# TensorE's queue order in a fused attention and mixture kernel: the attention product of a group placed behind the scores of the group four further on

## The chip, the cores and the metric

The kernel runs as one program on one core of a Trainium2 chip. The metric is the device time of one execution in microseconds (us); several executions are timed and the median is given. One further execution was recorded by the hardware profiler, and all rows below come from that one.

## The reference

Three stages follow each other. Attention with a top-k mask: for each of 4 batches and 8 heads, with 576 positions of width 64, only the 32 largest scores of a row stay.

```python
scores = scale * np.matmul(q, k.transpose(0, 1, 3, 2))
kth = np.partition(scores, -top_k, axis=-1)[..., -top_k:-top_k + 1]
scores = np.where(scores >= kth, scores, -1000000000.0)
attn = softmax(scores);  x = np.matmul(attn, v)
```

Then a dense block over the 2304 tokens: `h = x @ w_in` (512 to 2048), softplus, `@ w_out` (2048 to 512). Then a mixture of 8 experts of which each token takes one: `argmax` of `x @ w_gate`, and for the chosen expert `relu(x @ w1[e]) @ w2[e]` times the gate's probability.

## The kernel before, in words

Part one (`part_one`) does attention and the dense block interleaved, part two (`part_two`, from about 805 us of the profile on) the experts. Part two and the end of the dense block are not touched.

Attention is cut into 72 **groups** of two tiles, each tile 128 query rows of one head (or 64 and 64 rows, a "tail"). Two neighbouring heads of a batch are a pair; a pair's queries, keys and values sit in one of 4 buffers. A group j goes through these steps:

- **Scores**, `emit_qk`, L372 on TensorE: 8 to 12 matmuls into the PSUM tile `s`, of which there is one buffer. ScalarE copies it to SBUF (L380).
- **Softmax with top-k**, `emit_softmax`: VectorE folds the row into halves and quarters (L408 to L424; L424 is the last reader of the PSUM tile, so it sets the scores of group j+1 free), finds the 32nd largest value with pairs of L428 and L432, and makes the mask (L443, or L440, which multiplies at once). GpSimd multiplies by the mask (L444), ScalarE and GpSimd write the two float16 halves of the weights into `p16` (L448 to L450), and the SP queue transposes them by DMA into `pT` (L452). There are six `pT` buffers, the tiles of three groups.
- **The attention product**, `emit_av`, L467 and L469 on TensorE: 14 matmuls per tile with `pT` as the weights into the PSUM tile `m`, of which there is one buffer. VectorE makes the reciprocal of the row sums (L491, L493) and ScalarE writes the scaled rows `x` (L495).

Of `x` a **unit** of two tiles of 128 tokens is made for the dense block: ScalarE and GpSimd split it into float16 halves `xh` (L514, L515), the SP queue transposes it into `xT` (L516), and 16 **steps** follow, each of 12 matmuls of the first layer (L554) and 2 of the second (L588, or L585 for the last unit, recorded as two each). Behind a unit stands the routing of its tokens (L592 to L656).

What sets the order: the Python loop of `part_one` writes, at turn i, the scores of group i+1, the softmax of group i, the product of group i-3 (`LAG = 3`) and one or two steps of the dense block. A list scheduler then places all instructions on the five engines by priority and by a simulated time line. `tc.high_priority(offset=A_AV)` around the product (A_AV = 150; the scores have 100) lets it go ahead of much that was written earlier. Each engine executes its own list strictly in the order that results, and stops at an instruction whose operands are not there.

The scheduler places a product on TensorE as soon as it holds the transposed weights to be there. In the list that results product j stands mostly behind the scores of group j+2, with one group's turn between the end of its softmax and its place.

The names that the change and the steps of the prediction touch: `last_qk`, `emit_qk` (L372), `emit_av` (L467 to L495), the loop at the end of `part_one`.

Of the kernel before, what the change touches and what calls it, by code (L numbers as in the profile page):

```python
# [19 lines left out]
B, H, S, D = 4, 8, 576, 64  # L20
# [54 lines left out]
A_AV = 150  # L75
# [12 lines left out]
def attn_moe_moe2(ctx, tc, q, k, v, w_in, w_out, w_gate, w1, w2, out):  # L88
# [64 lines left out]
    def run(halves):  # L153
        nc.vector.memset(done, 0.0)
        with ExitStack() as p:
            late = part_one(tc, p, q, k, v, w_in, w_out, const, ident, before, ones, iota_e, reg_e, wg, ids,
                            ohcum, done, early, table, rows, flags if halves else None, sums, w_sums)
        with ExitStack() as p:
            part_two(tc, p, w1, w2, out, ident, ones, ohcum, done, early, late, table, rows, check if halves else None)
# [10 lines left out]
def part_one(tc, ctx, q, k, v, w_in, w_out, const, ident, before, ones, iota_e, reg_e, wg, ids,  # L170
             ohcum, done, early, table, rows, flags, sums, w_sums):
    nc = tc.nc
# [100 lines left out]
    def decode_some(n):  # L273
        for _ in range(n):
            if dec_q:
                f, *a = dec_q.pop(0)
                f(*a)
# [6 lines left out]
    def prep_load(m):  # L284
        b, hp = pairs[m]
        src = []
        bd = sm.tile([128, 3], F32, name="bd") if flags is None else sums[:, m]
        for i, x in enumerate((q, k, v)):
            t = raw.tile([128, R * D], F32, name="qkv"[i] + "n")
            nc.sync.dma_start(t, x[b, 2 * hp:2 * hp + 2].rearrange("h (p r) d -> (h p) (r d)", r=R))  # L290
            src.append(t)
        pair[m] = (src, bd)
        if flags is None or m >= LATEJ:
            magnitudes(m)
# [7 lines left out]
    def prep_scale(m):  # L302
        b = pairs[m][0]
        src, bd = pair[m]
        if flags is not None:
            return
        up, iv = pow2(all_sum(bd, ps_m, "m"), "m")
        sc = sm.tile([128, 8], F32, name="sc", bufs=KVB + 2)
        nc.vector.tensor_copy(sc[:, 0:3], up)
        nc.vector.tensor_tensor(out=v_up[:, b:b + 1], in0=v_up[:, b:b + 1], in1=up[:, 2:3], op=ALU.min)  # L310
        nc.vector.scalar_tensor_tensor(sc[:, 3:4], iv[:, 0:1], 1.0 / D ** 0.5, iv[:, 1:2],
                                       op0=ALU.mult, op1=ALU.mult)
        nc.vector.tensor_scalar(sc[:, 4:5], sc[:, 3:4], -1.0, None, op0=ALU.mult)
        for i in (1, 0, 2):
            nc.scalar.activation(src[i], src[i], AF.Copy, scale=sc[:, i:i + 1])
        pair[m] = (*src, sc)
# [36 lines left out]
        pair[m] = (q1, q2, kt, v16, sc)  # L353

    sc_t, pt_t, o_t, x_t = {}, {}, {}, {}
    tops = [None]

    def emit_qk(m, kind, ps, base):
        q1, q2, kt, v16, sc = pair[m]
        if kind == "tail":  # L360
            parts = [(8, 9, h, 64 * h, 64 * h + 64) for h in range(2)]
        else:
            t, h = kind
            parts = [(2 * t, 2 * t + 2, h, 0, 128)]

        cut = (512 * (base // 512 + 1) - base) // D
        for r0, r1, h, p0, p1 in parts:
            cs = slice(h * 64, h * 64 + 64)
            for qs, first in ((q1, True), (q2, False)):
                lhs = qs[:, h, r0:r1, :].rearrange("p r d -> p (r d)")  # L370
                for k0, k1 in ((0, cut), (cut, R)):
                    nc.tensor.matmul(ps[p0:p1, base + k0 * D:base + k1 * D], lhsT=lhs, rhs=kt[:, k0:k1, cs],  # L372
                                     start=first, stop=not first)

    def emit_scores(gi):
        s = row.tile([128, 2, S], F32, name="s")
        ps = ps_s.tile([128, 1536], F32, name="s")
        for i, x in enumerate(groups[gi]):
            emit_qk(*x, ps, i * S)
        nc.scalar.activation(s.rearrange("p i c -> p (i c)"), ps[:, 0:2 * S], AF.Copy)  # L380
        sc_t[gi] = s, ps
# [78 lines left out]
    def emit_av(m, kind):  # L460
        b, hp = pairs[m]
        v16, sc = pair[m][3:5]
        pT = pt_t.pop((m, kind))
        def products(o, pT, h):
            for r in range(R):
                c = r if r < 5 else r - 5
                nc.tensor.matmul(o[:, h, 0:D + 1], lhsT=pT(r), rhs=v16[:, h, c, 0:D + 1], start=r == 0, stop=r == R - 1)  # L467
                if r < 5:
                    nc.tensor.matmul(o[:, h, 0:D], lhsT=pT(r), rhs=v16[:, h, c, D + 2:], start=False, stop=False)  # L469

        def out_tile():
            return ps_m.tile([128, 512], F32, name="m")[:, :2 * D + 4].rearrange("p (h c) -> p h c", h=2)

        if kind == "tail":
            o = out_tile()
            p0 = 64 * (b % 2)
            for h in range(2):
                products(o[p0:p0 + 64], lambda r: pT[:, r, h * 64:h * 64 + 64], h)
            xt, ps_ = x_tile((b // 2, "tail%d" % (b // 2))), slice(p0, p0 + 64)
        else:  # L480
            t, h = kind
            if h == 0:
                o_t[m, t] = out_tile()
            o = o_t[m, t]
            products(o, lambda r: pT[:, r, :], h)
            if h == 0:
                return
            del o_t[m, t]
            xt, ps_ = x_tile((b, t)), slice(0, 128)
        rc = sm.tile([128, 2, 1], F32, name="rc")  # L490
        nc.vector.tensor_scalar(rc[ps_], o[ps_, :, D:D + 1], ESC * 1e-9,  # L491
                                2.0 ** -X_UP if flags is not None else sc[ps_, 2:3], op0=ALU.add, op1=ALU.mult)
        nc.vector.reciprocal(rc[ps_], rc[ps_])  # L493
        for h in range(2):
            nc.scalar.activation(xt[ps_, hp, h], o[ps_, h, 0:D], AF.Copy, scale=rc[ps_, h])  # L495
# [103 lines left out]
    def some_work(k):  # L599
        for _ in range(k):  # L600
            moe_step()
            if side:
                next(side[0], None)
                if side[0].gi_frame is None:
                    side.pop(0)
# [113 lines left out]
    pairs, tiles, first = [], [], []  # L719
# [18 lines left out]
    n = len(groups)  # L738
# [4 lines left out]
    for i in range(-1, n + LAG):  # L743
        if i == -1:
            with tc.high_priority(offset=AHEAD):
                for m in range(RB):
                    prep_load(m)
                prep_scale(0)
        while done_prep < len(pairs) and when[done_prep] <= i:
            with tc.high_priority(offset=A_PREP):  # L750
                if to_scale:
                    prep_scale(to_scale.pop()[0])
                prep_split(done_prep)
                if done_prep + RB < len(pairs):
                    prep_load(done_prep + RB)
                if done_prep + 1 < len(pairs):
                    to_scale.append((done_prep + 1, i + SCALE))
            done_prep += 1
        if to_scale and to_scale[0][1] <= i:
            with tc.high_priority(offset=AHEAD):  # L760
                prep_scale(to_scale.pop()[0])
        if i == -1:
            decode_some(2)
        if i + 1 < n:
            with tc.high_priority(offset=A_SC):
                emit_scores(i + 1)
        if 0 <= i < n:
            with tc.high_priority(offset=AHEAD):
                emit_softmax(i)
            with tc.high_priority(offset=0):  # L770
                decode_some(DECR)
        j = i - LAG
        if j >= 0:
            with tc.high_priority(offset=A_AV):
                for x in groups[j]:
                    emit_av(*x)
            for u in units.get(j, []):
                started += 1
                ready.append((u, started))
        if ready or cur or behind or side:  # L780
            credit += MOER
            some_work(int(credit))
            credit -= int(credit)
# [267 lines left out]
```

## Time and profile before

| | us |
|---|---|
| median of 3 runs | 1141.56 |
| lowest and highest run | 1136.7, 1143.85 |
| the profiled execution's own time | 1135.44 |
| its span, first to last instruction | 1133.7 |
| mean granted TensorE clock, share of full | 0.929 |

Three stretches can be told apart. Up to about 250 us the kernel also decodes the dense block's weights on VectorE, ScalarE and GpSimd. From 250 to about 805 us the rest of attention runs with the dense block beside it. From 805 us on come the last units and the experts, in which TensorE is busy throughout. The view "busy time by stretch" shows how much an engine does in a stretch, the view of waits what it stood still for, and the time line which instruction stood and which one ran on.

### The profile page before, as it was taken

To read this page: it belongs to the slowest core of one execution; us is meant where nothing else is said; L and a number is where in the kernel's file an instruction comes from. 1 tells how busy PE (TensorE), PEld (TensorE's weight loads), DVE (VectorE), ACT (ScalarE), POOL (GpSimd) and SP (SyncE) were. 2 spreads that over 40 slices of the span, in tenths; PEclk is the share of its full clock that TensorE was granted. 3 is DMA by queue.
4 is the path that set the end of the run, shared out by engine and by line. 5 is a ranking of instruction groups with operands and counts; after the bars stand their busy time and mean duration, and the time that the engine had idled before them with its cause. 6 is when DMAs were issued, how large, how long until landed. Compare 5 with 4: busy or idle time off the path is not lost. (4 is left out here: it accounts for less than half of the span.)

```text
span 1133.7 us, 22612 instructions
## 1 busy us (share of the span) xinstructions
PE 902.4 (80%) x7146; PEld 648.5 (57%) x7146; DVE 951.6 (84%) x2980; ACT 800.5 (71%) x1898; POOL 638.4 (56%) x731
## 2 busy tenths in 40 slices
PE   1233367757898797789988998998999999999992
PEld 0122244434565464556655565665678889999981
DVE  4998999999898897799988998999656787677771
ACT  6776688877677778687987776867679655555561
POOL 3986898987666677566767765656434112111110
PEclk9995589877999999899999998999999999999996
DMA  8897778975748877546769543354521566766650
GB/s 194 190 199 157 148 166 197 205 157 112 98 100 131 147 117 148 91 63 102 140 146 134 93 78 71 73 73 92 188 39 21 105 248 201 249 221 235 211 188 18
DMA packets 295880, 157.18 MB, mean 139 GB/s; under 512 B 257524, under 2 KB 257652, under 8 KB 295732
## 3 DMA queue, kind: packets, MB, share of 16 engines
q1 hardware_dynamic: 292116, 145.73, 60.1%
q0 software_dynamic: 3616, 9.72, 2.5%
q8 instruction: 62, 1.02, 0.4%
q14 instruction: 86, 0.70, 0.3%
HBM read 77.89 MB, written 11.11 MB: 79 GB/s over the span
## 5 line engine op out<-in xcount | busy, mean ns | idle before, releaser
L588 PE MATMUL y<-w_out_s,g 128*128 128x512 f32 x480 | 238.8, 618 | 11.3 <-POOL g L563 11.3
L554 PE MATMUL h<-xT,w_in_s 128*128 128x256 f16 (+1 forms) x1920 | 231.5, 270 | 9.1 <-ACT g L560 4.7
L554 PEld LDWEIGHTS <-w_in_s 128*128 128x128 f16 x1920 | 173.4, 101 | 77.0 <-issue 52.9
L432 DVE MAX8 mx<-wk 128x8 f32<-128x144 f32 (+2 forms) x432 | 198.5, 493 | 0.1
L467 PE MATMUL m<-v,pT 128*128 128x65 f16 (+1 forms) x1440 | 104.5, 203 | 103.4 <-DMA pT<-p 88.1
L563 POOL TENSOR_TENSOR g<-g,sa 128x256 f32<-128x256 f32 (+1 forms) x160 | 118.3, 741 | 108.2 <-ACT sa L562 95.9
L450 POOL TENSOR_TENSOR p<-e,p 128x512 f16<-128x512 f32 x144 | 169.1, 1174 | 0.0
L372 PE MATMUL s<-kt,q 128*128 128x512 f16 (+7 forms) x640 | 104.3, 326 | 76.9 <-DVE wk L424 52.2
L467 PEld LDWEIGHTS <-pT 128*128 128x128 f16 (+1 forms) x1440 | 91.4, 108 | 120.3 <-DMA pT<-p 107.5
L444 POOL TENSOR_TENSOR e<-e,mk 128x576 f32<-128x576 f32 x84 | 110.9, 1322 | 63.5 <-DVE mk L443 47.7
L428 DVE MATCH_REPLACE8 wk<-mx,wk 128x144 f32<-128x144 f32 (+1 forms) x432 | 144.3, 339 | 0.1
L448 ACT ACTIVATE p<-e 128x576 f16<-128x576 f32 x144 | 98.1, 682 | 53.3 <-DVE e L440 19.5
L588 PEld LDWEIGHTS y<-w_out_s,g 128*128 128x128 f32 x480 | 84.1, 198 | 73.1 <-issue 54.1
L870 POOL DMA_INDIRECT out_dram<-ot,idx x19 | 19.8, 1045 | 177.8 <-DVE ot L869 159.2
L372 PEld LDWEIGHTS <-q 128*128 128x128 f16 (+1 forms) x640 | 46.7, 110 | 124.5 <-issue 47.9
L890 PEld LDWEIGHTS h<-xT,wf 128*128 128x128 f32 x864 | 111.9, 191 | 5.3 <-ACT wf L851 0.2
L890 PE MATMUL h<-xT,wf 128*128 128x256 f32 x864 | 114.0, 283 | 0.0
L903 PE MATMUL y<-wf,hT 128*128 128x512 f32 x432 | 112.6, 398 | 0.0
L421 ACT ACTIVATE e<-s,bias 128x576 f32<-128x576 f32 x144 | 105.6, 770 | 1.6 <-POOL p L450 0.8
L380 ACT ACTIVATE s<-s 128x1152 f32<-128x1152 f32 x72 | 81.0, 1125 | 6.6 <-PE s L372 6.4
L903 PEld LDWEIGHTS y<-wf,hT 128*128 128x128 f32 x432 | 76.7, 189 | 13.2
L469 PE MATMUL m<-v,pT 128*128 128x64 f16 (+1 forms) x800 | 80.4, 203 | 0.0
(193 smaller groups left out, 1907.3 us busy)
## 6 DMA issues: line engine op xcount, KB each, us to landing
w1r<-in_moe_w_dram SPq DMA_DIRECT2D x20, 1024.0 KB, 5.1
w2r<-in_moe_w_dram SPq DMA_DIRECT2D x20, 1024.0 KB, 6.5
w<-in_moe_w_in_dram SPq DMA_DIRECT2D x16, 512.0 KB, 5.2
w<-in_moe_w_out_dram SPq DMA_DIRECT2D x16, 512.0 KB, 4.3
rows<-xr SPq DMA_DIRECT2D x37, 128.2 KB, 2.5
qn<-in_q_dram SPq DMA_DIRECT2D x16, 288.0 KB, 3.2
kn<-in_k_dram SPq DMA_DIRECT2D x16, 288.0 KB, 3.2
vn<-in_v_dram SPq DMA_DIRECT2D x16, 288.0 KB, 3.3
```

Source lines behind the costliest of these rows:

```text
L372: nc.tensor.matmul(ps[p0:p1, base + k0 * D:base + k1 * D], lhsT=lhs, rhs=kt[:, k0:k1, cs], start=first, stop=not first)
L421: nc.scalar.activation(e[i], s[i], AF.Exp, bias=bt[:, i], scale=SCORE if flags is not None else sc[i][:, 3:4])
L428: nc.vector.match_replace(out=to, in_to_replace=mx[:, i, 8 * j:8 * j + 8], in_values=src[i], imm_value=NEG)
L432: nc.vector.max(out=mx[:, i, 8 * j + 8:8 * j + 16], in_=src[i])
L444: nc.gpsimd.tensor_tensor(out=e[i], in0=e[i], in1=mk, op=ALU.mult)
L450: nc.gpsimd.tensor_tensor(out=p16[:, S + D:], in0=e[i][:, 0:S - D], in1=p16[:, 0:S - D], op=ALU.subtract)
L467: nc.tensor.matmul(o[:, h, 0:D + 1], lhsT=pT(r), rhs=v16[:, h, c, 0:D + 1], start=r == 0, stop=r == R - 1)
L554: nc.tensor.matmul(hps[:, :n], lhsT=w_in_s[:, c, j, p, o:o + 128], rhs=xT[:, 0:len(u.tiles), r, c, :], start=m == 0, stop=m == 3 * KD - 1)
L563: nc.gpsimd.tensor_tensor(out=g, in0=g, in1=a[:, :n], op=ALU.add)
L588: nc.tensor.matmul(u.y[i], lhsT=g[:, cs], rhs=w_out_s[:, f, :], start=f == 0, stop=f == KF - 1)
L890: nc.tensor.matmul(h, lhsT=w1f[:, a, c, :], rhs=xT[:, b, c, :], start=n == 0, stop=n == 3 * KD - 1)
L903: nc.tensor.matmul(y[i], lhsT=hT[g][:, a, i * 128:i * 128 + 128], rhs=w2f[:, b, :], start=g == 0 and n == 0, stop=g == KF2 - 1 and n == 2)
```

## The change

The product of group j = i-3 is now issued behind the last score matmul of group i+1 = j+4 on TensorE: `emit_qk` keeps its latest matmul in `last_qk`, and the block that writes the product is entered with `tc.issue_after(...)`. That adds an edge for order alone from that matmul to each instruction of the block on the same engine; no semaphore is added by it. Products 68 to 71 have no scores four further on (the loop's test `i + 1 < n`) and stand behind the last ones. Nothing is computed otherwise.

```diff
-    tops = [None]
+    tops, last_qk = [None], [None]
...
-                    nc.tensor.matmul(ps[p0:p1, base + k0 * D:base + k1 * D], lhsT=lhs, rhs=kt[:, k0:k1, cs],
-                                     start=first, stop=not first)
+                    last_qk[0] = nc.tensor.matmul(ps[p0:p1, base + k0 * D:base + k1 * D], lhsT=lhs,
+                                                  rhs=kt[:, k0:k1, cs], start=first, stop=not first)
...
-            with tc.high_priority(offset=A_AV):
+            with tc.high_priority(offset=A_AV), ExitStack() as behind_scores:
+                if i + 1 < n:
+
+                    behind_scores.enter_context(tc.issue_after(last_qk[0].ins))
                 for x in groups[j]:
                     emit_av(*x)
```

The scheduler makes a new list for every engine from this. Three places follow; line numbers are those of the kernel in which the rows stand, and up to L771 they are the same in both.

**TensorE at group 59.** `s_8773` are the scores of group 61, `s_9076` those of group 63, `pT_8701` the transposed weights of group 59's first tile. Before:

```order
L372 MATMUL s_8773<-kt_8338,q2_8337 128x128
L616 MATMUL h_10358<-ident_61,xr_9904 128x128 x4
L467 LDWEIGHTS pT_8701
L467 MATMUL m_9133<-v16_8062,pT_8701 128x65
L469 LDWEIGHTS pT_8701
L469 MATMUL m_9133<-v16_8062,pT_8701 128x64
```

and after the change:

```order
L372 LDWEIGHTS q2_7605
L372 MATMUL s_9076<-kt_7606,q2_7605 64x128
L467 LDWEIGHTS pT_8701
L467 MATMUL m_9133<-v16_8062,pT_8701 128x65
L469 LDWEIGHTS pT_8701
L469 MATMUL m_9133<-v16_8062,pT_8701 128x64
```

The product of group 59 stood behind the scores of group 61 and now stands behind those of group 63. Over all groups: of products 0 to 67, 61 stood behind the scores of the group two further on and 7 behind those of the group three further on; now all stand behind the fourth.

**VectorE at the same group.** `rc_9162<-m_9133` reads product 59; `wk_8937` belongs to the softmax of group 61, `e_9090` and `mk_9118` to that of group 62. Before:

```order
L424 TENSOR_TENSOR wk_8937<-s_8773,s_8772 128x2x288
L414 MAX mx_8783<-wk_8937 128x8 x2
L491 TENSOR_SCALAR rc_9162<-m_9133 128x2
L428 MATCH_REPLACE wk_8937<-mx_8783,wk_8937 128x144 x2
L493 RECIPROCAL rc_9162<-rc_9162 128x2
```

and after the change:

```order
L440 SCALAR_TENSOR_TENSOR e_9090<-s_8918,mx_8783,e_9090 128x576
L443 TENSOR_SCALAR mk_9118<-s_8918,mx_8783 128x576
L628 MAX_INDEX ix_10475<-m8_10473,lg_10471 128x8
L630 TENSOR_SCALAR nm_10477<-m8_10473 128x1
L491 TENSOR_SCALAR rc_9162<-m_9133 128x2
L408 TENSOR_TENSOR s_9076<-s_9076,s_9075 128x288
```

The first reader of product 59 moved from the middle of softmax 61 to the end of softmax 62, behind all of its rounds and its mask.

**TensorE behind the last scores.** The first product that stands behind the scores of group 71 is that of group 69 before (`pT_10130`):

```order
L554 LDWEIGHTS w_in_s_150
L554 MATMUL h_11117<-xT_10732,w_in_s_150 128x256
L467 LDWEIGHTS pT_10130
L467 MATMUL m_10509<-v16_7618,pT_10130 128x65
L469 LDWEIGHTS pT_10130
```

and that of group 67 after the change (`pT_9816`):

```order
L588 MATMUL y_10862<-w_out_s_151,g_11010 128x512
L588 MATMUL y_10863<-w_out_s_151,g_11010 128x512
L467 LDWEIGHTS pT_9816
L467 MATMUL m_10277<-v16_8350,pT_9816 128x65
L469 LDWEIGHTS pT_9816
```

Between the last scores and the end of product 71 there stood 78 matmuls of L554, 14 of L588 and six tiles of products; now 108, 18 and ten. Behind the end of product 71 TensorE's list is the same in both kernels.

## Rows read from the trace of the kernel before

**Rows 1.** The page: busy time by engine, share of the span, instructions

```profile
PE 902.4 (80%) x7146; PEld 648.5 (57%) x7146; DVE 951.6 (84%) x2980; ACT 800.5 (71%) x1898; POOL 638.4 (56%) x731
```

**Rows 2.** By stretch: PE, PEld, DVE, ACT, POOL busy; clock, DMA share, GB/s

```profile
0.00:250.00 250.00, 113.31 (x931) 67.47 (x932) 231.15 (x642) 184.41 (x391) 202.44 (x207) 0.83 0.84 182
250.00:805.00 555.00, 486.96 (x4194) 318.30 (x4192) 504.17 (x1816) 421.15 (x1044) 369.10 (x449) 0.95 0.61 104
```

**Rows 3.** Waits of VectorE, 250 to 805 us: total, times, longest

```profile
DVE rc L491 <- PE m L467: 24.5, 11, 5.7
DVE s L408 <- ACT s L380: 7.7, 7, 3.0
DVE lg L624 <- PE h L622: 3.8, 4, 2.4
```

**Rows 4.** Waits of TensorE, 250 to 805 us

```profile
PE m L467 <- DMA pT<-p: 36.2, 21, 6.0
PE m L467 <- ACT x L495: 9.7, 6, 3.3
```

**Rows 5.** Time line of TensorE, 676 to 696 us: start, length, instructions [wait before]

```profile
677.81 1.14 PE L372 MATMUL s<-kt,q 128*128 128x512 f16 x8
...
684.74 0.24 PE L467 MATMUL m<-v,pT 128*128 128x65 f16 x1 [5.35 <-DMA pT<-p]
...
685.50 2.75 PE L554 MATMUL h<-xT,w_in_s 128*128 128x256 f16 x12
...
691.40 1.36 PE L554 MATMUL h<-xT,w_in_s 128*128 128x256 f16 x11
692.69 1.29 PE L372 MATMUL s<-kt,q 128*64 128x512 f16 x12
```

**Rows 6.** Time line of VectorE, the same stretch

```profile
675.99 0.75 DVE L424 TENSOR_TENSOR wk<-s 128x576 f32<-128x576 f32 x1
...
682.77 0.46 DVE L408 TENSOR_TENSOR s<-s 128x288 f32<-128x288 f32 x1
...
690.71 0.16 DVE L491 TENSOR_SCALAR rc<-m 128x2 f32<-128x2 f32 x1 [5.04 <-PE m L467]
```

**Rows 7.** The view of Rows 2, for the stretch behind that wait

```profile
684.70:688.50 3.80, 3.76 (x27) 2.91 (x28) 0.97 (x3) 0.84 (x2) 1.42 (x2) 0.50 0.10 21
```

**Rows 8.** Waits in the first 250 us, TensorE and VectorE

```profile
PE m L467 <- DMA pT<-p: 51.9, 14, 7.8
...
DVE rc L491 <- PE m L467: 0.3, 1, 0.3
```

**Rows 9.** Busy time by stretch, last scores to end of product 71

```profile
777.20:804.40 27.20, 24.80 (x195) 15.24 (x193) 26.92 (x129) 17.87 (x46) 19.12 (x25) 1.00 0.47 86
```

**Rows 10.** Time line of TensorE, 796 to 803 us

```profile
796.09 1.47 PE L554 MATMUL h<-xT,w_in_s 128*128 128x256 f16 x12
797.40 1.88 PE L588 MATMUL y<-w_out_s,g 128*128 128x512 f32 x4
...
802.42 0.20 PE L467 MATMUL m<-v,pT 128*128 128x65 f16 x1
```

**Rows 11.** Time line, 711 to 715 us: from a product's rows to transposed x

```profile
711.39 0.50 ACT L495 ACTIVATE x<-m,rc 128x64 f32<-128x64 f32 x2
...
714.41 1.68 SPq L516 DMA_TRANSPOSE xT<-xh  x1
```

**Rows 12.** Landing times of the DMAs of L516

```profile
DMA to landing us min/median/max: 3.0/3.5/10.3
```

**Rows 13.** Time line, 656 to 671 us: VectorE and SP, group 58

```profile
656.60 0.75 DVE L424 TENSOR_TENSOR wk<-s 128x576 f32<-128x576 f32 x1
...
669.30 1.31 SPq L452 DMA_TRANSPOSE pT<-p  x1
```

**Rows 14.** VectorE by form, 250 to 805 us: busy, mean ns of one

```profile
L443 DVE TENSOR_SCALAR mk<-s,mx 128x576 f16<-128x576 f32 x53 | 34.0, 641 | 0.1
```

**Rows 15.** The same form, 30 to 250 us

```profile
L443 DVE TENSOR_SCALAR mk<-s,mx 128x576 f16<-128x576 f32 x30 | 26.8, 903 | 0.0
```

## The prediction, made before the changed kernel was run

> **What bounds the kernel now.** I read the busy time of the engines first, then busy time by stretch, then the waits of the two busiest engines, then the time line at one wait. Over the whole span VectorE is the busiest engine with 84%, TensorE has 80% [rows 1]. That mean mixes three stretches. In the first 250 us VectorE is busy for 231.15 us and TensorE for 113.31; from 250 to 805 us VectorE has 504.17 of 555 us, TensorE 486.96 [rows 2]. So VectorE sets the pace of attention, TensorE comes close behind it, and both stand still for part of the middle stretch: VectorE for 50.8 us, TensorE for 68.0. Those 50.8 us are what any change of order in the middle stretch can give.
>
> The largest part has one cause. VectorE waited 24.5 us, 11 times, at L491, the first reader of a product, for TensorE's L467 [rows 3]; TensorE itself waited 36.2 us, 21 times, at L467 for transposed weights that the DMA had not landed [rows 4]. The time line shows one of these: TensorE finished the scores of group 61 at about 678.9 us, stood 5.35 us before product 59, and then still had steps of the dense block and the other tile ahead of the next scores at 692.69 [rows 5]. VectorE came to L491 meanwhile and stood 5.04 us [rows 6]. The wait of one engine became the wait of both.
>
> **The change part by part.** It adds no arithmetic, no DMA and no semaphore of its own; it moves the small matmuls of products 0 to 67 later in TensorE's list, and the scheduler moves their readers with them.
>
> *The wait for transposed weights.* Product j moves from behind scores j+2 (seven times j+3) to behind scores j+4. Scores j+4 cannot start before L424 of group j+3 has read PSUM. So the weights get one or two turns of a group more, at 504.17 / 52 = 9.7 us of VectorE's work each; the longest wait here was 6.0 us [rows 4]. I take the wait as gone. Bounds: nothing goes, or all 36.2 us on TensorE.
>
> *Its reader on VectorE.* At group 59 L491 now stands at the end of softmax 62, where the time from L424 to there was 6.8 us in the softmax before it (675.99 to 682.77) [rows 6]. TensorE needs, from the same L424, some 1.3 us of scores [rows 5] and two tiles of a product, under 1 us. So VectorE should find the product done, by some 4 us. The 24.5 us go.
>
> *Other waits behind it.* VectorE also stood 7.7 us at L408 for the copied scores and 3.8 us at L624 for the routing matmuls [rows 3]; both come late when TensorE is held. Some are TensorE's ordinary load. Between nothing and 11.5 us I take half, 5.8, since the time line shows one such delay and I cannot assign the rest.
>
> *The first 250 us.* TensorE waited 51.9 us there for transposed weights, and VectorE only 0.3 us at L491 [rows 8]. This is covered by VectorE's decoding: I take nothing. If that cover were gone, these waits would count too.
>
> *What comes back at the end.* From the last scores to the end of product 71 were 27.20 us, of which TensorE was busy 24.80 [rows 9]. Its list now has there 30 more matmuls of L554, four more of L588 and four more tiles. A step of 12 and 2 takes (802.42 - 796.09) / 2 = 3.17 us, the first 12 of it 1.31 [rows 10]; so 30 x 0.109 = 3.3, 4 x 0.93 = 3.7, and four tiles at under 0.5 us make 2.0: 9.0 us. 24.80 + 9.0 = 33.8 us is longer than the 27.20, so TensorE's work sets this end and 6.6 us return. Lower bound nothing, if VectorE is late in any case; upper bound 9.0. What is late next is thus TensorE itself, behind the last scores.
>
> *Transposed x for a unit.* Products end later, and the scheduler left the first steps of a unit closer behind them: for the second unit one group of scores lies between, with no step. From the start of L495 to the issue of L516 were 3.0 us [rows 11], and a landing takes 3.5 us in the median, 10.3 at most [rows 12]. L495 follows L491, 7.5 us after its L424; so x is there about 14 us after it, at worst 21. TensorE comes to the step after the next L424 (9.7 us), scores and a tile: 11.5 us. It waits 2.5 to 9.3 us, and the next scores stand behind that. They have at most 6.8 - 1.3 = 5.5 us to spare before VectorE's L408, less ScalarE's copy, so VectorE pays 0 to 5 us. I take 2, nearer to the median landing.
>
> *SP and the six buffers.* Product j must be done before the transposes of group j+3 can be written. I take nothing; the rival below prices it.
>
> **The sum.** -24.5 - 5.8 + 6.6 + 2.0 = -21.7 us. On the profiled execution's 1135.44 that gives 1113.7; the median shown, 1141.56, lies 6.1 above that execution, and from it the sum gives 1119.9. I predict **1120 us**.
>
> **The rivals.**
>
> *TensorE becomes the bound.* Its 486.96 us of the middle stretch must fit into what is left. In the dense stretch at the end it was busy 24.80 of 27.20, 0.912 [rows 9]; in the middle 0.877. At 0.912 the stretch would take 534 us, 21 less, as in my sum; halfway, at 0.895, it takes 544, 11 less: 1131 us, and less gain if lower. For it: both engines are near full and each must wait for the other once per group. Against it: 45.9 of the 68.0 idle us are waits at the products [rows 4].
>
> *Masks collide with GpSimd.* L443 took 641 ns in the mean from 250 us on, and 903 ns where GpSimd decodes [rows 14, 15]. With 53 of them, 53 x 0.262 = 13.9 us would come back if the new order brought the second mean: 1134 us. Against it: GpSimd's work in the middle stretch stays at 369.10 us. The Trainium skill ("SBUF — State Buffer", section "SBUF: two separate sides") has a rule for this: VectorE and GpSimd share a pair of ports, and whichever starts second is fully blocked. By that rule the loss hangs on how the two lists meet, which the edge does not steer.
>
> *The six buffers come back too late: slower.* Where two steps stand between scores j+4 and the end of product j, some 20 groups in the new list, the product ends 1.3 + 2 x 3.17 + 0.9 = 8.5 us after L424 of group j+3. The second transpose of a group started 12.0 us after its L424 (657.35 to 669.30) [rows 13]. The margin is 3.4 us. If TensorE is later than that, SP stops at L452 with all that is queued behind it, ScalarE stops for a free `p16`, and VectorE for its scores. At the 5.0 us of rows 6 that is 20 x 1.6 = 32 us: 1120 + 32 = 1152; at 6.0 us it is 52: 1172. Decisive is whether TensorE is more than 3.4 us behind VectorE as a rule. For it: VectorE has little slack left. Against it: what made TensorE that late was the wait that goes.
>
> *A colder TensorE: slower.* Behind the wait of 5.35 us the granted clock was 0.50, the level of 1.2 GHz, for 3.8 us [rows 7], and 12 matmuls of L554 took 2.75 us, where 11 took 1.36 a little later [rows 5]. Such a stretch costs 1.9 us. If TensorE now stood at the scores of every group as long, 52 x 1.9 = 99 us would exceed its 68.0 idle us by 31: 1173 us. Against it: without the waits at the products, (68.0 - 45.9) / 52 = 0.4 us of idle TensorE are left per group. The Trainium skill ("TensorE: Matmul & The Clock Gate", section "Why this matters for your kernels") warns of idle gaps between bursts of matmuls, and tying products to scores makes such gaps where VectorE is slow; rows 7 agree that a gap is paid for afterwards.
>
> That the change does not do what it says is excluded by the list.
>
> **How the numbers follow.** Forecast 0.66 (about 1101 to 1130); TensorE bound 0.17 (1131 to 1142); masks 0.05 (1134); buffers 0.08 (1152 to 1172); cold clock 0.04 (1173). About 1% can be told from no change here, that is 1130 and 1153. Faster 0.66; same 0.17 + 0.05 = 0.22; slower 0.08 + 0.04 = 0.12. The low end takes all three rows of VectorE's waits, 36.0 us, with nothing given back, from the lowest run: 1136.7 - 36.0 = 1101. The high end takes in the two cases without a gain: 1143. Left out are the slower cases, 0.12, and a larger gain.
>
> **What would show it.** In the changed kernel's profile: TensorE's wait at L467 for `pT` from 250 us on under 5 us; VectorE's wait at L491 under 5 us; VectorE's idle time in attention down from 50.8 to about 25 us; the last scores some 28 us earlier but product 71 only 21 to 22 us, with TensorE busy throughout between them; the rest of the span as long as before. Wrong would be: SP waiting at L452 for TensorE (buffers), a granted clock below 0.95 in the middle (cold clock), a mean of L443 towards 900 ns (masks), or VectorE waiting at L408 for L380 for more than 15 us (TensorE bound).

## The result, and the profile after

| | before | after |
|---|---|---|
| median, us | 1141.93 (4 runs) | 1125.28 (4 runs) |
| lowest to highest | 1136.70 to 1143.85 | 1115.34 to 1129.23 |
| profiled execution, own time | 1135.44 | 1126.11 |
| its span | 1133.7 | 1124.4 |

The ratio of after to before is 0.9839, with a 95% interval of 0.9802 to 0.9876: 16.7 us less on the medians, where 21.7 were forecast. The two profiled executions differ by 9.3 us only, since that of before lies 6.5 us below its median and that of after 0.8 above. So the traces account for 9.3 us, and 7 us more lie in the spread of the executions, which no trace here takes apart. All that follows is measured on the 9.3.

The page first: busy time by engine, as in [rows 1]. TensorE and VectorE have 6.5 and 3.2 us less, and the instructions are as many.

```profile
PE 895.9 (80%) x7146; PEld 646.0 (57%) x7146; DVE 948.4 (84%) x2980; ACT 798.7 (71%) x1898; POOL 638.0 (57%) x731
```

Busy time by stretch, with the columns of [rows 2]. The first stretch is as before. In the second the busy time of VectorE grew by 1 us and that of TensorE by 3.6, in the same 555 us; the granted clock is 0.95 again.

```profile
0.00:250.00 250.00, 110.41 (x956) 67.77 (x956) 232.42 (x639) 187.21 (x399) 201.93 (x207) 0.85 0.83 182
250.00:805.00 555.00, 490.57 (x4208) 320.16 (x4209) 505.13 (x1847) 421.97 (x1056) 373.81 (x454) 0.95 0.63 110
```

A fixed window holds other work before and after, so I also measured from the same instruction to the same instruction: from the end of L424 of group 19 to that of group 71 ("middle"), from there to the last matmul of product 71 ("end"), and the rest.

| us | before | after | difference | forecast |
|---|---|---|---|---|
| start to L424 of group 19 | 247.9 | 246.7 | -1.2 | 0 |
| middle | 538.7 | 523.8 | -14.9 | -28.3 |
| end | 17.8 | 27.2 | +9.4 | +6.6 |
| rest | 329.3 | 326.7 | -2.6 | 0 |
| VectorE idle, middle | 50.5 | 41.7 | -8.8 | |
| TensorE idle, middle and end | 68.2 | 65.6 | -2.6 | |

The last row is the one to keep in mind: the waits for transposed weights were to leave TensorE, and its idle time hardly fell.

The middle is 14.9 us shorter, but VectorE's idle time fell by 8.8 us only. The other 6.1 us are busy time of VectorE (third figure of the rows below, before and after), for which the sum had no term. Part of it is work that now lies outside the two marks, 1718 instructions for 1726; part are the same instructions in less time, such as the two of L575 (1.71 us each before, 0.68 after).

```profile
247.90:786.60 538.70, 472.80 (x4071) 309.38 (x4072) 488.15 (x1726) 410.44 (x1017) 359.32 (x436) 0.95 0.62 105
246.70:770.50 523.80, 460.61 (x3975) 300.06 (x3975) 482.11 (x1718) 402.66 (x999) 355.58 (x433) 0.95 0.63 108
```

The waits of TensorE from 250 to 805 us, to be set beside [rows 4]; columns are total, times, longest. The 36.2 us for `pT` are gone without a row. In their place stand 28.1 us at the second layer for `g`, which GpSimd finishes, and 10.1 us at the first layer for the transposed x.

```profile
PE y L588 <- POOL g L563: 28.1, 11, 7.1
PE h L554 <- DMA xT<-xh: 10.1, 3, 5.0
PE m L467 <- ACT x L495: 6.6, 5, 2.7
PE h L616 <- ACT xr L592: 6.4, 4, 2.8
PE h L554 <- ACT g L560: 5.0, 5, 1.5
```

The same view of the kernel before had these two for `g`, which the prediction did not look at:

```profile
PE y L588 <- POOL g L563: 6.9, 5, 4.5
PE h L554 <- ACT g L560: 3.4, 3, 2.8
```

The waits of VectorE in the same stretch, beside [rows 3]. L491 still has 16.6 us; L408 is where it was, only in more and shorter pieces; L624 has no row any more, but L440 and L636 have grown.

```profile
DVE rc L491 <- PE m L467: 16.6, 7, 5.5
DVE gs L636 <- ACT ex L635: 7.9, 5, 2.7
DVE e L440 <- ACT e L421: 7.6, 5, 4.2
DVE s L408 <- ACT s L380: 7.3, 12, 1.6
```

Product 59, which [rows 5, 6] showed waiting, now runs right behind the scores of group 63 and without a wait. First TensorE's time line, then VectorE's (start, length, instruction): L491 comes at 692.14 in the place that the order gave it, behind the mask L443, and waits for nothing.

```profile
689.73 1.27 PE L372 MATMUL s<-kt,q 128*128 128x512 f16 x12
690.94 0.20 PE L467 MATMUL m<-v,pT 128*128 128x65 f16 x1
...
691.51 0.51 DVE L443 TENSOR_SCALAR mk<-s,mx 128x576 f16<-128x576 f32 x1
...
692.14 0.15 DVE L491 TENSOR_SCALAR rc<-m 128x2 f32<-128x2 f32 x1
```

The longest wait at L491 that is left, at 375.81 us, has another cause. TensorE (first two rows) stood 5.00 us before the first layer of a unit whose transposed x SP had issued at 362.76 (third row); that is 5.8 us from issue to the matmul. The first tile of the product for L491 stood behind those 24 matmuls, its second tile behind the scores that follow (fourth row), and VectorE stood 5.48 us.

```profile
361.53 1.98 PE L588 MATMUL y<-w_out_s,g 128*128 128x512 f32 x4
368.51 5.18 PE L554 MATMUL h<-xT,w_in_s 128*128 128x256 f16 x24 [5.00 <-DMA xT<-xh]
...
362.76 2.87 SPq L516 DMA_TRANSPOSE xT<-xh  x1
...
374.05 0.42 PE L372 MATMUL s<-kt,q 128*64 128x512 f16 x2
...
375.81 0.16 DVE L491 TENSOR_SCALAR rc<-m 128x2 f32<-128x2 f32 x1 [5.48 <-PE m L467]
```

From the last scores to the end of product 71, beside [rows 9]: 35.10 us for 27.20, of which TensorE is busy 32.73. The same seven L491 waits include one of 5.47 us here, at 797.83; so 11.1 us of the 16.6 lie in the middle, where 24.5 were.

```profile
762.60:797.70 35.10, 32.73 (x292) 21.70 (x291) 29.07 (x145) 21.92 (x61) 19.74 (x26) 1.00 0.45 85
```

### The profile page after: what moved, and what is told of

Read it like the earlier page. It is cut to its first block, busy times and chain, and to the rows that moved or that the text cites. A ratio compares the mean times of both kernels' runs of the same rounds, so it can differ in the third digit from the quotient of the medians.

```text
span 1124.4 us, 22653 instructions
## 1 busy us (share of the span) xinstructions
PE 895.9 (80%) x7146; PEld 646.0 (57%) x7146; DVE 948.4 (84%) x2980; ACT 798.7 (71%) x1898; POOL 638.0 (57%) x731
## 4 chain that ended last, share of the span: by engine, by line
PE 34%; DVE 28%; DMA 13%; issue 8%; POOL 7%; ACT 6%; SPq 2%; POOLq 0%; ACTq 0%; DVEq 0%
PE h L893 8%; PE y L906 8%; DVE mx L432 6%; PE h L554 5%; DVE wk L428 5%; PE y L588 4%; DMA pT<-p 4%; DVE xr L216 3%; DVE mk L443 2%; PE y L585 2%; POOL p L450 2%; DVE e L440 2%; DVE wk L424 2%; DMA w<-in_moe_w_in_dram 1%; POOL g L563 1%
## 5 line engine op out<-in xcount | busy, mean ns | idle before, releaser
L588 PE MATMUL y<-w_out_s,g 128*128 128x512 f32 x480 | 244.2, 634 | 31.3 <-POOL g L563 31.0
L554 PE MATMUL h<-xT,w_in_s 128*128 128x256 f16 (+1 forms) x1920 | 226.6, 268 | 23.4 <-DMA xT<-xh 10.1
L554 PEld LDWEIGHTS <-w_in_s 128*128 128x128 f16 x1920 | 173.6, 101 | 95.3 <-issue 60.3
L372 PE MATMUL s<-kt,q 128*128 128x512 f16 (+7 forms) x640 | 97.8, 315 | 131.5 <-DVE wk L424 87.7
L448 ACT ACTIVATE p<-e 128x576 f16<-128x576 f32 x144 | 98.2, 684 | 73.6 <-DMA pT<-p 35.2
L588 PEld LDWEIGHTS y<-w_out_s,g 128*128 128x128 f32 x480 | 86.5, 201 | 101.8 <-issue 61.3
L421 ACT ACTIVATE e<-s,bias 128x576 f32<-128x576 f32 x144 | 105.8, 770 | 2.1 <-POOL p L450 0.9
L467 PE MATMUL m<-v,pT 128*128 128x65 f16 (+1 forms) x1440 | 92.3, 200 | 9.7 <-ACT x L495 8.4
L467 PEld LDWEIGHTS <-pT 128*128 128x128 f16 (+1 forms) x1440 | 85.5, 105 | 16.3 <-issue 12.5
L469 PE MATMUL m<-v,pT 128*128 128x64 f16 (+1 forms) x800 | 75.7, 200 | 0.0
```

What stands on the lines that cost most here:

```text
L372: last_qk[0] = nc.tensor.matmul(ps[p0:p1, base + k0 * D:base + k1 * D], lhsT=lhs, rhs=kt[:, k0:k1, cs], start=first, stop=not first)
L421: nc.scalar.activation(e[i], s[i], AF.Exp, bias=bt[:, i], scale=SCORE if flags is not None else sc[i][:, 3:4])
L554: nc.tensor.matmul(hps[:, :n], lhsT=w_in_s[:, c, j, p, o:o + 128], rhs=xT[:, 0:len(u.tiles), r, c, :], start=m == 0, stop=m == 3 * KD - 1)
L588: nc.tensor.matmul(u.y[i], lhsT=g[:, cs], rhs=w_out_s[:, f, :], start=f == 0, stop=f == KF - 1)
```

## The experiments

Each kernel is the changed one with the edit shown, unless the edit says otherwise; line numbers of those with `last_of` are one higher from L382 on. To make room in SBUF, several let the `x` tiles of the tails share one buffer under one name ("xtail"); no run has that edit alone. A ratio goes by the kernel before as timed beside the kernel in question, whose median lay between 1140.73 and 1145.27 us, so the ratios can be compared and the medians only roughly. The table sums the waits from 250 to 805 us of each profiled execution: "pT" is L467 for the transposed weights, "g" the sum of L588 for `g` and L554 for L560, "rc" VectorE at L491, "idle" VectorE's idle time in the middle.

| kernel | median us | ratio to before, interval | pT | g | rc | idle |
|---|---|---|---|---|---|---|
| before | 1141.93 | 1 | 36.2 | 10.3 | 24.5 | 50.5 |
| the change | 1125.28 | 0.9839, 0.9802 to 0.9876 | 0 | 33.1 | 16.6 | 41.7 |
| behind 3 | 1129.40 | 0.9857, 0.9810 to 0.9903 | 3.7 | 33.3 | 9.2 | 39.3 |
| seven pT | 1130.05 | 0.9866, 0.9836 to 0.9895 | 0 | 39.8 | 16.1 | 46.4 |
| middle only | 1131.18 | 0.9891, 0.9864 to 0.9919 | 0 | 34.5 | 13.6 | 40.8 |
| first only | 1140.54 | 0.9976, 0.9953 to 0.9999 | 39.8 | 10.2 | 35.6 | 47.6 |
| low priority | 1141.15 | 1.0012, 0.9980 to 1.0044 | 15.8 | 15.6 | 12.3 | 52.5 |
| own zeros | 1127.43 | 0.9862, 0.9830 to 0.9893 | 0 | 37.9 | 13.7 | 46.8 |
| behind 3, own zeros | 1122.32 | 0.9841, 0.9805 to 0.9878 | 1.3 | 32.8 | 4.2 | 33.8 |
| third step | 1116.65 | 0.9771, 0.9726 to 0.9816 | 0 | 22.9 | 3.0 | 26.2 |
| third step alone | 1133.03 | 0.9906, 0.9871 to 0.9941 | 21.6 | 22.2 | 25.4 | 54.1 |
| third step, behind 3 | 1124.58 | 0.9851, 0.9812 to 0.9890 | 0.7 | 34.9 | 10.7 | 41.8 |
| fourth step | 1136.41 | 0.9933, 0.9903 to 0.9964 | 0 | 32.1 | 19.7 | 43.3 |
| third step, x earlier | 1118.25 | 0.9789, 0.9728 to 0.9850 | 0 | 24.0 | 3.6 | 27.0 |

**Behind three groups instead of four.**

```diff
+        last_of[gi] = last_qk[0].ins
...
-                if i + 1 < n:
-                    behind_scores.enter_context(tc.issue_after(last_qk[0].ins))
+                if j + 3 < n:
+                    behind_scores.enter_context(tc.issue_after(last_of[j + 3]))
```

> The product of group j stands behind the scores of group j+3 instead of j+4. Theory (the gain is the wait for transposed weights, and one turn more is enough for them; the second turn only costs): TensorE's wait at L467 for pT from 250 us on stays under 6 us, SP's wait at L452 for TensorE falls from 23.1 us to under 5, and of the 9.4 us that came back behind the last scores about half do not, so 1113 to 1120 us. Rival A (the weights need both turns): the wait for pT is back at 15 us or more, 1130 to 1138 us. Rival B (any new list moves the time by a per cent, the place of the product is not the cause): no relation, anything from 1112 to 1142 us with waits for pT that don't follow the time.

0.9857, not to be told from the change, and not the 1113 to 1120 us of the theory. SP's wait at L452 for TensorE fell to 0.4 us, as expected. One group's turn more than before is nearly enough for the weights (3.7 us left); the second turn bought nothing that shows.

**A seventh pT buffer.** It tests the rival of the buffers. In the changed kernel SP did wait at L452 for TensorE, which it had not before, and ScalarE waited twice as long at L448 (35.2 us; 17.7 before):

```profile
SPq L452 <- PE m L467: 23.1, 12, 5.2
```

```diff
-             pT = row.tile([128, R, 128], F16, name="pT", bufs=2 * LAG)
+             pT = row.tile([128, R, 128], F16, name="pT", bufs=2 * LAG + 1)
```

> The change, with seven pT buffers instead of six (room for it comes from one buffer shared by the two tail tiles of x, whose lives don't overlap). Theory (part of the gain is given back because a product now returns its pT buffer so late that SP stops at L452 and ScalarE at L448): SP's wait at L452 for TensorE falls from 23.1 us to under 10, ScalarE's at L448 for pT from 35.2 us to about 20, and the time falls by 3 to 8 us against the change, 1117 to 1122 us. Rival (these waits lie beside VectorE's work): the waits fall and the time stays at 1125 us, within 3.

With seven buffers SP's wait at L452 for TensorE has no row any more, ScalarE's falls to 25.6 us, and the kernel is not faster (0.9866), as the rival had it. The stops of SP were real, and cost nothing that shows.

**The edge for the products of one stretch only.** The first kernel has it for products 17 to 67, the second for 0 to 16.

```diff
-                if i + 1 < n:
+                if 19 < i < n - 1:
```

```diff
-                if i + 1 < n:
+                if i <= 19:
```

> The edge only for products from group 17 on (the middle stretch), the first 17 as before. Theory (the gain is made from 250 us on; in the first 250 us VectorE's decoding covers every wait of TensorE): the whole gain, 1122 to 1129 us. Rival (the first stretch has a part in it, by steps done earlier or later): half of it, 1130 to 1137 us.

> The edge only for products 0 to 16, the others as before. Theory (no gain is made in the first 250 us): 1138 to 1145 us, and the waits of before return from 250 us on, about 36 us of TensorE at L467 for pT and 20 to 25 us of VectorE at L491. Rival (a new list as such gives the gain): 1120 to 1130 us.

0.9891 and 0.9976. Most of the gain, 1.1% of 1.6%, belongs to the middle, as the prediction had it. In us the first kernel falls into the rival's range (1131.18), but beside a kernel before that was 3.3 us slower, and its interval overlaps that of the change: whether the first stretch has a part in the rest is not shown. What the first stretch gives by itself, 0.24% or some 2.7 us, is hardly to be told from nothing: its interval ends at 0.9999. In the trace of the second kernel the waits of the middle are back, and those of VectorE at L491 are longer than they were:

```profile
PE m L467 <- DMA pT<-p: 39.8, 12, 6.5
...
DVE rc L491 <- PE m L467: 35.6, 14, 7.2
```

**Later by priority, without the edge.**

```diff
-A_AV = 150
+A_AV = 0
...
-                if i + 1 < n:
-                    behind_scores.enter_context(tc.issue_after(last_qk[0].ins))
```

> No edge; the product's priority offset is 0 instead of 150. The list then has 37 products behind the scores of the group two further on, 18 behind the third and 13 behind the fourth. Theory (the place in the list is the cause, however it comes about): TensorE's wait at L467 for pT from 250 us on falls with the share of moved products, from 35 us to some 15 to 22, and the gain against before is a third to a half of the change's 1.6%, a ratio of 0.990 to 0.995. Rival (the edge matters by something else than the place): no gain, 1.000.

1.0012: no change, where the theory gave 0.990 to 0.995. The scheduler put 37 of the products behind the scores two further on, 18 behind three and 13 behind four. The wait for pT fell to 15.8 us and that at L491 to 12.3, and VectorE's idle time did not fall (52.5). Two waits were about halved and nothing came of it: VectorE stood elsewhere, 12.2 us at L408, 9.6 at L636, 7.7 at L440 for L421 and 6.2 at L624. So the wait for pT, taken by itself, does not tell the gain.

**Own zeros.** In the changed kernel GpSimd waited 9.62 us at L667, where a buffer of `xr` is cleared that a store still read, and TensorE's longest wait at L588 came with it (GpSimd's time line, then TensorE's):

```profile
310.37 0.52 POOL L667 MEMSET xr<- 128x513 f32 x1 [9.62 <-DMA rows<-xr]
310.86 0.71 POOL L563 TENSOR_TENSOR g<-g,sa 128x256 f32<-128x256 f32 x1
...
311.63 3.78 PE L588 MATMUL y<-w_out_s,g 128*128 128x512 f32 x4 [7.06 <-POOL g L563]
```

```diff
-        z = x2p.tile([128, ROWW], F32, name="xr")
-        nc.gpsimd.memset(z, 0.0)
+        with tc.issue_after(scatters[-1].ins):
+            nc.gpsimd.memset(z := wp.tile([64, ROWW], F32, name="zt"), 0.0)
```

> The change, with the 64 rows of zeros of the late tokens (L667) cleared in a tile of their own, at the same place of GpSimd's queue, instead of in a buffer that a DMA still reads; the two tail tiles of x share a buffer for the room. Theory (GpSimd's stop of 9.6 us at L667 in the changed kernel, which held L563, L444, ScalarE's L448 and VectorE's L440, is a loss that the new list brought by chance): the stop is gone and the time falls by 4 to 8 us against the change, a ratio to before of 0.977 to 0.981. Rival (VectorE makes the time up in the groups that follow): ratio 0.984, within 0.002.

> As the kernel before this one, with the product behind the scores of group j+3. Theory (one turn more is enough for the weights, and costs less at the units' first steps and at the buffers): ratio to before 0.974 to 0.980, no more than the version with j+4. Rival (VectorE's idle time has other causes by now): 0.983 to 0.986.

The stop at L667 is gone, and the time is that of the change: 0.9862, and 0.9841 for the second kernel, which also puts the product behind three groups (0.9857 by itself). Both theories, 0.981 at most, fell, and the figures lie at or near those of the rivals. The largest single wait of a list was not worth taking out; 26.1 us at L588 are still there in the first.

**A third step between the layers.** `GLAG` is how many steps the second layer trails the first. With three, TensorE reaches L588 a step of 3.17 us later ([rows 10]).

```diff
-GLAG = 2
+GLAG = 3
```

> The change, with the second layer of the dense block three steps behind the first instead of two (GLAG 3, one more buffer of g; the tail tiles share a buffer for the room). Theory (the products' wait was replaced by TensorE's wait at L588 for GpSimd's g, 28.1 us against 6.9 before, and that costs): the wait falls to under 10 us and the ratio to before to 0.974 to 0.981. Rival (that wait lies beside VectorE's work, which sets the pace): the wait falls and the ratio stays at 0.984, within 0.003.

0.9771: the fastest of all. TensorE's wait at L588 is halved, if not under the 10 us expected, and VectorE's at L491 nearly gone:

```profile
PE y L588 <- POOL g L563: 14.3, 10, 4.1
PE h L554 <- DMA xT<-xh: 9.8, 3, 6.6
PE h L554 <- ACT g L560: 8.6, 8, 2.3
...
DVE rc L491 <- PE m L467: 3.0, 3, 1.8
```

VectorE's idle time in the middle is 26.2 us and its wait at L491 3.0: the 25 and under 5 that the prediction gave for the change alone. The middle takes 511.2 us, 27.5 less than before (28.3 were forecast).

**The third step without the edge, with the product behind three groups, and a fourth step.** The first is the kernel before with `GLAG = 3`; the second has the edit of "behind three" besides; the third has `GLAG = 4`.

```diff
-GLAG = 2
+GLAG = 4
```

> The kernel before, without the edge, in which the second layer (L588) trails the first by three steps instead of two. Theory: TensorE's 28.1 us at L588 for g are what the edge brought (the kernel before had 6.9 us there), so the longer distance gives little by itself: 1134 to 1145 us, with TensorE's wait at L467 for pT still over 15 us and VectorE's at L491 over 12 us. Rival: the third step is a gain of its own that has nothing to do with the edge, and gives the same 10 us here as on top of the edge: 1128 to 1134 us.

> Three steps of distance for the second layer, and the product behind the scores of the group three further on instead of four. Theory: the wait at pT is gone already one group earlier, the wait at L588 with the third step, and the products lie one group nearer to the last scores, so that the end gives back less: 1110 to 1116 us, L467 for pT under 5 us. Rival: what one group of distance gives is not more than what two give, as before without the third step (1129.4 against 1125.3): 1117 to 1121 us.

> The change, with the second layer four steps behind the first. Theory: most of the 28.1 us at L588 went with the third step already (14.3 left), and ScalarE and GpSimd, which make g, are late by a fixed time, so the fourth step takes the wait under 7 us and VectorE's idle time in the middle stretch under 24 us, but more of the dense block lies behind the last scores (131 matmuls of L554 for 101): 1112 to 1119 us. Rival: the wait at L588 is set by ScalarE's and GpSimd's load, not by distance; it stays at 12 us or more and the kernel gets slower by the work behind the last scores: 1120 to 1126 us.

The third step alone gives 0.9906, so it is a gain of its own, as the rival had it, and about additive: 0.9906 times 0.9839 is 0.9747, inside the interval of 0.9771. How it gains there stays open: its profiled execution (1137.07) lies 4 us above its median and shows VectorE's waits as before.

```profile
PE m L467 <- DMA pT<-p: 21.6, 14, 3.8
PE y L588 <- POOL g L563: 12.5, 6, 6.5
...
DVE rc L491 <- PE m L467: 25.4, 14, 4.7
```

With the product behind three groups the third step adds nothing (0.9851 against 0.9857): L588 has 15.9 us, but L554 for L560 has 19.0. The theory fell there, and 1124.58 lies above the rival's 1121 as well. The fourth step loses what the third gained (0.9933), beyond the 1120 to 1126 us of the rival: L588 stays at 15.2, L554 for L560 has 16.9, L491 is back, and from the last scores to the end of product 71 are 38.6 us (32.7 with three steps).

```profile
PE h L554 <- ACT g L560: 16.9, 6, 6.8
PE y L588 <- POOL g L563: 15.2, 8, 4.1
...
DVE rc L491 <- PE m L467: 19.7, 12, 3.5
```

**Is the third step's gain one lucky list?** In the program the transposed x is asked for two steps earlier.

```diff
-GLAG = 2
-XAHEAD = 2
+GLAG = 3
+XAHEAD = 4
```

> The change with the second layer three steps behind the first (1116.65 us by itself), and with the transposed x of the next unit asked for four steps before it is needed instead of two; that moves under a tenth of TensorE's list. Theory: the gain of the third step belongs to the distance and does not hang on the rest of the list, so 1112 to 1120 us, with TensorE's wait at L588 for g under 16 us and VectorE's at L491 under 6 us; the wait for xT (9.8 us there) may shrink by a few us. Rival: 1116.65 was one favourable list among many, as the fourth step (1136.41) and the product behind three groups (1124.58) suggest; then a small change of order loses it: 1123 to 1134 us, with waits at L491 of over 10 us again.

0.9789, with 13.8 us at L588, 3.6 at L491 and 27.0 us of VectorE's idle time. But the question stays open, for the edit moved nothing: in the traces of the two kernels with the third step every engine has the same instructions in the same order, by line, tile name and shape, 7146 on TensorE and 2980 on VectorE. So this is the third step timed a second time, and it gives the same to 0.2%. Whether another list with the third step would give it too no run shows, and the two neighbours that have other lists, behind three groups and with a fourth step, did not. Why x is late is open for the same reason: the wait for xT, 9.8 us in both, was not put to a test.

## Why the prediction was right, and where it was not

**The sign, the range and the first step held; what that step was to give came by half.** The waits of TensorE for transposed weights from 250 us on are gone, the edge for the middle products makes most of the gain, and 1125 lies in 1101 to 1143. Of the signs that the prediction named, the wait at pT came; L491 under 5 us, 25 us of idle VectorE, last scores 28 us earlier and TensorE busy throughout behind them did not. The gain forecast, 21.7 us, was 16.7 on the medians, but 9.3 on the traces, on which the sum was made: that 1125.28 lies so near to 1120 is in part luck of the executions.

*The 24.5 us at L491 and 5.8 more.* This is the step that was mis-sized. In the middle L491 fell by 13.4 us. From 250 to 805 us L408 fell by 0.4 and L624's 3.8 went, but L636 for L635 grew from 4.3 to 7.9 and L440 for L421 from 0.6 to 7.6. VectorE's idle time fell by 8.8 us where 28.3 were summed (30.3 less the 2.0 for transposed x). So the last scores ended 14.6 us earlier (762.6 for 777.2), not 28, and product 71 6.7 us earlier (797.7 for 804.4), not 21 to 22. The reasoning took TensorE's time from L424 to the end of the product from its work alone, 1.3 us of scores and under 1 us of product, as if TensorE stood for nothing else. But against the 36.2 us that left TensorE stand 22.8 more at `g` and 10.1 at xT, and its idle time fell by 2.6.

Had the waits for `pT` covered these waits, in that ScalarE and GpSimd made `g` while TensorE stood at a product? The table looks like it: in the three kernels with over 20 us at pT the waits for `g` are 10 to 22 us, and in those with under 4 us they are 32 to 40, but for the two that have the third step and the edge behind four. The traces, step by step, bear it out for a small part only. In the kernel before, TensorE stood at products between the first and second layer in 61 of the 115 steps whose second layer lies from 250 to 805 us; without these waits, and all else as it was, it would have come ahead of `g` at ten steps, by 4.6 us in all (an estimate from that trace). On the mean TensorE came from the first layer of a step to its second in 9.50 us before and 8.92 after, half of the difference being less work between them; and `g` itself was made in 6.47 us before and 6.99 after. The five longest waits for `g` after the change make 23.3 of the 28.1 us. In two, at 311.63 and 352.89 us, `g` came late: 14.1 and 14.0 us after its first layer, where the same steps had taken 4.6 and 3.7. In the first of these GpSimd stood at L667, in the second ScalarE stood 4.53 us at L330. In the other three `g` had taken about as long before (27.8, 20.3 and 13.9 us for 34.2, 17.0 and 13.4), and TensorE came 3.7 to 11.3 us sooner. The `g` of the first in the kernel before, and the stop of ScalarE in the second after the change:

```profile
304.45 0.74 POOL L563 TENSOR_TENSOR g<-g,sa 128x256 f32<-128x256 f32 x1
...
347.06 0.68 ACT L330 ACTIVATE st<-qn 128x576 f16<-128x576 f32 x1 [4.53 <-DMA kt<-st]
```

So the new waits are partly waits that had been there to be met, and partly waits that the new lists brought. That the waits for `g` held VectorE back in the change is suggested by the third step on top of it: 10.2 us less of them, 15.5 us less of idle VectorE. It is not proved: the third step gains without the edge as well, and the sum of such waits does not order all the kernels ("low priority" has 31 us of pT and `g` together and gains nothing). What decides how much of a wait taken out comes back stays open; that most of it did is measured.

*Transposed x.* Priced at 2.0 us; one wait of 5.00 us on TensorE cost VectorE 5.48 at once, with a landing of 5.8 us, a little over the 0 to 5 us that the worst landing gave, which was reckoned at 10.3 us. The value taken went by the median landing; the wait that counted was at the longest one.

*The end.* 6.6 us were to come back, with TensorE as the bound of this stretch: 33.8 us of work. It took 35.10, TensorE being busy 32.73 of them: 7.9 us came back from the last scores, 9.4 from L424 of group 71. The mechanism held and the size is short by a few us, since TensorE stood still for 2.4 us there too.

*The first 250 us.* Nothing was taken, and L424 of group 19 ended 1.2 us earlier. The waits for `pT` left TensorE there as well (51.9 us in [rows 8]) and its waits for L424 of VectorE grew from 46.1 us to 85.1, the cover that the prediction named; L491 has 0.2 us:

```profile
PE s L372 <- DVE wk L424: 85.1, 15, 11.3
...
DVE rc L491 <- PE m L467: 0.2, 1, 0.2
```

**The rivals.** *Buffers:* their sign appeared, 23.1 us of SP at L452, and the seventh buffer showed that it costs nothing. *TensorE as the bound:* L408 did not grow (7.3 us for 7.7), but the rival's core, that each engine must now and then wait for the other, is what is left: TensorE's idle time stayed. Its price of 11 us less gain is nearer to the middle stretch (13.4 us less gain than forecast) than the forecast's own. It was argued away by counting 45.9 of 68.0 idle us as waits at the products, as if they had nothing behind them. *Masks:* L443 took 615 ns in the mean from 250 us on, and 929 before that, as in [rows 14, 15]:

```profile
L443 DVE TENSOR_SCALAR mk<-s,mx 128x576 f16<-128x576 f32 x53 | 32.6, 615 | 0.0
...
L443 DVE TENSOR_SCALAR mk<-s,mx 128x576 f16<-128x576 f32 x31 | 28.5, 929 | 0.0
```

*Cold clock:* 0.95 in the middle, as before. It shows only behind single waits, as [rows 7] did: the 24 matmuls at 368.51 us took 5.18 us, and the granted clock in the stretch behind that wait was half of full, 1.2 GHz:

```profile
368.40:371.40 3.00, 2.89 (x14) 2.10 (x15) 1.94 (x9) 0.79 (x2) 2.60 (x3) 0.50 0.71 138
```

## What to carry to other kernels

A wait that is taken out of an engine's strict order does not come off its idle time one for one: the engine comes sooner to what stands next, and the new order makes other operands late. Before its time is booked as a gain, look through the rest of that engine's waits and ask which of them it would meet next, and at what price. Compare the engine's total idle time before and after, not the row of the wait; here that row fell by 36.2 us and the idle time by 2.6. And before a new wait is called one that had been covered, look at when its operand was made before and after. Then try the distance that goes with the next wait: moving the product and giving the second layer one step more were worth 2.3% together, where each alone gave 1.6% and 0.9%, and one step more again lost most of it. Such a gain belongs to the lists that were run, until another list shows it too.

## What was not expected of the hardware

Executions of one list spread more than the effect of many edits: the change ran from 1115.34 to 1129.23 us, the last kernel from 1107.63 to 1120.57, each on one order of instructions. A profiled execution lay up to 6.6 us from the median of its kernel, on either side (1135.44 against 1141.93 before, 1136.67 against 1130.05 with seven buffers). A sum made against one trace carries that much of error before any term is wrong.
